# Loading a fused attention and gMLP kernel in smaller pieces: x tiles one by one, q weights in four blocks, k weights between two halves of x block 1

## The chip, the cores and the metric

The kernel runs on one core of a Trainium2 chip. The metric is the time of one execution on the device in microseconds (us). Five runs of the kernel before are at hand, and one execution recorded by the hardware profiler.

The engines are named as in the profile: PE is TensorE's matmul, PEld its weight load, DVE is VectorE, ACT is ScalarE, POOL is GpSimd, SP is SyncE (it only issues transfers here). A trailing q (SPq, ACTq) is an engine's instruction queue.

## What is computed

One input x (2048 tokens of 512 features, bf16) is normalised, and the sum of x, a local attention branch and a gated MLP branch is returned.

```python
xn = layernorm(x)                                   # over 512 features
# A: 32 heads of 16; each token attends to 8 tokens, 2 apart, itself and back
q, k, v = split(xn @ wqkv)                          # wqkv: 512 x 1536
attn = softmax(mask(q . k[pos - 2*w] * 16**-0.5), over w = 0..7)
A = (sum over w of attn * v[pos - 2*w]) @ wo
# B: gMLP with a token-mixing matrix
z = gelu(xn @ w_in)                                 # 512 x 1376, two halves of 688
z2 = layernorm(z[:, 688:])
B = (z[:, :688] * (w_sp @ z2 + b_sp)) @ w_out       # w_sp: 2048 x 2048
out = x + A + B
```

## The kernel before

The 2048 tokens stand as 16 tiles of 128 tokens. Tile i = 4*tb + j belongs to block j (0 to 3) and to row group tb (0 to 3), so a block is four tiles that are 512 tokens apart. `xall[:, j, tb]` holds tile (j, tb) of x, tokens on the partitions. A tile goes through these steps:

- `ln_stats` (L205, L206, DVE): mean and variance of each token.
- `ln_sqrt` (L209, ACT) and `ln_recip` (L212, DVE): 1/sqrt(var + eps).
- `ln_apply` (L216, DVE): the normalised tile, in place.
- transposed into `xnT` (features on the partitions): either `tr` (L223, four PE transposes into PSUM) and `tr_copy` (L227, ACT), or `tr_dma` (L231, a transposing transfer issued by SP). Block 0 and the first two tiles of block 1 go through PE, the other ten tiles by DMA.

`qk_part(pq, j, m, b0, b1)` (L308) then multiplies the transposed tiles b0 to b1 of block j with a quarter of the q or k weights: m = 0, 1 are the q weights `wqk[:, 0]`, m = 2, 3 the k weights `wqk[:, 1]`. `qk_copy` (L318, ACT) casts a finished product to SBUF, where DVE multiplies q with shifted k (L342). The products for z follow at L237.

The order of instructions on PE, DVE, ACT, SP and POOL is written out by hand (`manual_schedule`). In the opening part, the lines L557 to L641 give it; from there on the token list `ORDER` gives it, and the change touches nothing in that list. The framework adds the waits. It also gives the transfers eight completion semaphores in turn, in the program's order: the ninth transfer uses the first one again, and its issuing queue waits until the older transfer has landed.

What the opening does, in the program's order:

- Loads (L171 to L180). Tiles 0 and 1 of block 0 come as column halves of 64 KB, the left ones issued by SP, the right ones by ACT. ACT then issues tiles 2 and 3 of block 0 as one transfer of 256 KB. SP issues the q weights (512 KB), block 1 of x (512 KB), the k weights (512 KB), blocks 2 and 3 of x, and the z2 weights `w_z2` (688 KB).
- `warm_up` (L550): ten matmuls on zeros while the first data arrive, two more after the first transposes.
- Tiles 0 and 1 of block 0 are normalised and transposed, then tiles 2 and 3.
- PE multiplies q for tiles 0 and 1 (the products `pqs[0]`, `pqs[1]`), with the transposes of tiles 2 and 3 between; then q for tile 2 alone (`qk_part(..., 2, 3)`, L583 and L584), then k for tiles 0 and 1 (`pqs[2]`, L585: the first use of the k weights), then q for tile 3 alone (L595).
- ACT copies `pqs[0]` and `pqs[1]` out, and then takes the square root for tiles 2 and 3 of block 1 (L597), which go through `ln_apply` and `tr_dma`.

Of the kernel before, what the change touches and what calls it, by code (L numbers as in the profile page):

```python
# [15 lines left out]
P = 128  # L16
S = 2048
D = 512
NT = S // P
TB = 4  # L20
TBS = 512
C = D // P
# [48 lines left out]
def kernel(  # L71
# [14 lines left out]
    A = nc.scalar  # L86
    G = nc.gpsimd
    PE = nc.tensor
    SP = nc.sync
# [3 lines left out]
    xblk = x2.rearrange("(b j p) d -> j p b d", b=TB, j=4)  # L93
# [9 lines left out]
    xall = r_x[:, 0:4 * TB * D].rearrange("p (j b d) -> p j b d", j=4, b=TB)  # L103
    vp = r_x[:].rearrange("p (d t) -> p d t", d=DH)
    r_w = sb.tile([P, 8192], BF16, name="r_w")
    wqk = r_w[:, 0:4096].rearrange("p (s k f) -> p s k f", s=2, k=C)
# [57 lines left out]
    def load_x0(E, tb, h):  # L164
        E.dma_start(xall[:, 0, tb, 256 * h:256 * h + 256], x2[tb * TBS:tb * TBS + P, 256 * h:256 * h + 256])

    def load_wqk(E, s):
        E.dma_start(wqk[:, s],
                    A_wqkv[:, s * D:(s + 1) * D].rearrange("(k p) f -> p k f", p=P))

    for tb in range(2):  # L171
        load_x0(SP, tb, 0)
        load_x0(A, tb, 1)
    A.dma_start(xall[:, 0, 2:4, :], xblk[0][:, 2:4, :])
    load_wqk(SP, 0)
    SP.dma_start(xall[:, 1], xblk[1])
    load_wqk(SP, 1)
    for j in range(2, 4):
        SP.dma_start(xall[:, j], xblk[j])
    SP.dma_start(w_z2[:], B_w_in[:, FH:F].rearrange("(k p) f -> p k f", p=P))  # L180
# [121 lines left out]
    def qk_part(pq, j, m, b0, b1, ccs=(0, 1), p0=None, kcs=range(C)):  # L302
        sd, c0 = m // 2, 2 * (m % 2)
        p0 = b0 if p0 is None else p0
        xv = xnT[:].rearrange("p k (b j t) -> p k b j t", b=TB, j=4)
        for cc in ccs:
            for kc in kcs:
                PE.matmul(pq[:, cc, p0 * P:(p0 + b1 - b0) * P], wqk[:, sd, kc, c0 + cc:D:C],  # L308
                          xv[:, kc, b0:b1, j, :], start=(kc == 0), stop=(kc == C - 1))

    def qk_copy(pq, j, m, b0=0, b1=TB, p0=None):
        sd, c0 = m // 2, 2 * (m % 2)
        p0 = b0 if p0 is None else p0
        if sd == 0:
            dst = qs[:, j, c0:c0 + 2, b0 * P:b1 * P].rearrange("p c (b t) -> p c b t", b=b1 - b0)
        else:
            dst = ks[:, c0:c0 + 2, HALO:HALO + S].rearrange("p c (b j t) -> p c b j t", b=TB, j=4)[:, :, b0:b1, j, :]
        cast = A.copy(dst, pq[:, :, p0 * P:(p0 + b1 - b0) * P].rearrange("p c (b t) -> p c b t", b=b1 - b0))  # L318
        if sd == 1:
            for i in k_reads[j]:  # L320
                tc.declare_no_dep(cast.ins, i, reason="other token columns of the same rows")
            k_casts[j].append(cast.ins)

    def qk_tile():
        return ps_mm.tile([P, 2, TBS], F32, name="pq", tag="mm")
# [250 lines left out]
    pqs = [qk_tile() for _ in range(3)]  # L576
# [3 lines left out]
    qk_part(pqs[1], 0, 1, 0, 2, (0,))  # L580
    tr_copy(t0[3], tr(t0[3]))
    qk_part(pqs[1], 0, 1, 0, 2, (1,))
    qk_part(pqs[0], 0, 0, 2, 3)  # L583
    qk_part(pqs[1], 0, 1, 2, 3)  # L584
    qk_part(pqs[2], 0, 2, 0, 2)  # L585
    for n in range(2):
        ln_stats(i1[n])
# [4 lines left out]
    ln_apply(i1[1])  # L592
    ln_stats(i1[3])
    for n in range(2):
        qk_part(pqs[n], 0, n, 3, 4)  # L595
        qk_copy(pqs[n], 0, n)
    ln_sqrt(slice(9, 16, 4))  # L597
    ln_stats(i2[0])
# [22 lines left out]
    pqs = [qk_tile() for _ in range(3)]  # L621
# [79 lines left out]
```

## Time and profile before

| what | value |
|---|---|
| median of 5 runs | 203.96 us (203.88 to 204.41) |
| the profiled execution: time, span of the instructions in it | 204.89 us, 203.2 us |
| granted TensorE clock | 1.000 |
| PE, DVE, ACT busy, share of the span | 97%, 92%, 49% |
| bytes read from HBM, written to it | 10.13 MB, 2.10 MB |
| q weights: issue, packets from and to, landed | 1.73, 2.87 to 6.07, 6.99 us |
| x tiles 2 and 3 of block 0 | 1.74, 3.56 to 6.49, 7.11 us |
| x block 1 | 2.20, 6.07 to 7.52, 8.61 us |
| k weights | 2.75, 7.53 to 9.01, 10.11 us |
| x block 2 | 3.31, 9.02 to 10.51, 11.62 us |
| x block 3 | 4.48, 10.53 to 12.05, 13.07 us |
| w_z2 | 5.08, 12.05 to 14.31, 14.89 us |

The transfers' times are those of the profiled execution, in microseconds from the first instruction: the start of the issuing instruction, the starts of the first and the last data packet (packets put to transfers by their order in the queue), and the last of the sixteen marks with which a transfer reports its landing. A row of a timeline or of the groups gives line, engine, operation, the names written and read, the shape and a count; brackets at its end give the idle time ahead of it and what ended it. PE rows overlap, since a matmul's time includes its way through the array: the pace is read from start to start.

### The profile page before, as it was taken

What the parts mean: (1) busy time and instruction counts of PE and PEld (TensorE: products, weight loads), DVE (VectorE), ACT (ScalarE), POOL (GpSimd) and SP (SyncE); (2) the same over time, 40 slices, a digit from 0 to 9 for tenths busy, and PEclk for the clock granted to TensorE, in tenths of its full rate; (3) what the DMA queues carried; (4) which work ended last, traced back from release to release, by engine and by line L of the source; (5) the groups of instructions that cost most, each with busy time, mean ns of one, the idle gap of its engine ahead of it and who ended that gap; (6) DMA issues with size and microseconds to landing.
All of it is one profiled execution on the core that took longest, in us unless ns stands there. A gap on an engine that the chain in (4) does not pass through costs nothing.

```text
span 203.2 us, 4070 instructions
## 1 busy us (share of the span) xinstructions
PE 196.9 (97%) x1687; PEld 125.0 (62%) x1691; DVE 187.1 (92%) x267; ACT 100.1 (49%) x162; POOL 11.5 (6%) x14
## 2 busy tenths in 40 slices
PE   7799999999999999999999999999999999999993
PEld 2498866565566666666556666666546645664562
DVE  5689899999999999999989998999999999999804
ACT  3466999999969984651642309647100210031000
POOL 3000000593000000000000000000000000000000
PEclk9999999999999999999999999999999999999999
DMA  4982448100198000687398966989927810744264
GB/s 130 361 270 53 89 99 206 60 0 3 42 193 181 3 0 0 114 205 171 30 219 200 189 169 105 205 163 162 183 50 194 212 43 0 216 102 93 55 194 135
DMA packets 66290, 25.91 MB, mean 128 GB/s; under 512 B 56224, under 2 KB 66016, under 8 KB 66016
## 3 DMA queue, kind: packets, MB, share of 16 engines
q1 hardware_dynamic: 65568, 25.19, 55.0%
q10 hardware_dynamic: 704, 0.47, 0.7%
q8 instruction: 13, 0.21, 0.5%
q14 instruction: 5, 0.04, 0.1%
HBM read 10.13 MB, written 2.10 MB: 60 GB/s over the span
## 4 chain that ended last, share of the span: by engine, by line
PE 89%; DMA 4%; DVE 2%; SPq 2%; issue 1%; ACTq 0%; DVEq 0%
PE pg L451 37%; PE pz L237 18%; PE pq L308 13%; PE pv L412 7%; PE po L523 6%; PE po L499 5%; DMA r_x<-in_A_x_dram 3%; SPq L476 1%; PE pl L362 1%; DVE r_qk L513 1%; DMA out_dram<-r_qk 1%; PE po L508 1%; DVE stats L205 1%; PE pt L223 1%; PE pa L308 0%
## 5 line engine op out<-in xcount | busy, mean ns | idle before, releaser
L451 PE MATMUL pg<-z,r_qk 128*128 128x344 bf16 x448 | 67.3, 309 | 0.0
L451 PEld LDWEIGHTS <-r_qk 128*128 128x128 bf16 x448 | 43.7, 98 | 22.4 <-issue 0.8
L237 PE MATMUL pz<-w_z,xnT 128*128 128x344 bf16 x256 | 40.1, 309 | 0.0
L426 DVE TENSOR_TENSOR r_pr<-r_x,r_w 128x2048 bf16<-128x2048 bf16 x32 | 38.3, 1221 | 0.3
L430 DVE TENSOR_TENSOR r_pr<-r_pr 128x2048 bf16<-128x2048 bf16 x28 | 33.9, 1219 | 0.2
L457 ACT ACTIVATE gs<-pg,b_col 128x688 bf16<-128x688 f32 x16 | 13.3, 832 | 40.6 <-PE pg L451 25.1
L237 PEld LDWEIGHTS <-xnT 128*128 128x128 bf16 x256 | 24.9, 98 | 13.4 <-issue 0.8
L308 PE MATMUL pq<-xnT,r_w 128*128 128x256 bf16 (+2 forms) x192 | 28.8, 304 | 0.2 <-DMA r_w<-in_A_wqkv_dram 0.2
L342 DVE TENSOR_TENSOR r_pr<-r_qk 128x2048 bf16<-128x2048 bf16 x24 | 28.5, 1222 | 0.0
L308 PEld LDWEIGHTS <-r_w 128*128 128x128 bf16 x200 | 20.2, 114 | 7.4 <-DMA r_w<-in_A_wqkv_dram 0.7
L299 ACT ACTIVATE r_uz<-pz 128x688 bf16<-128x688 f32 x16 | 11.5, 742 | 22.5 <-PE pz L237 22.3
L318 ACT CAST r_qk<-pq 128x1024 bf16<-128x1024 f32 (+1 forms) x16 | 15.3, 990 | 2.4 <-PE pq L308 2.3
L523 PE MATMUL po<-r_w,r_uz 128*128 128x512 bf16 x66 | 14.9, 379 | 0.6 <-issue 0.6
L513 DVE TENSOR_TENSOR r_qk<-po,r_qk 128x512 bf16<-128x512 f32 x14 | 9.2, 687 | 6.2 <-PE po L523 6.0
L412 PE MATMUL pv<-xnT,r_w 128*32 128x512 bf16 x256 | 14.6, 380 | 0.0
L499 PE MATMUL po<-r_lg,r_pr 32*128 32x512 bf16 x224 | 14.5, 375 | 0.0
L523 PEld LDWEIGHTS <-r_uz 128*128 128x128 bf16 x85 | 8.0, 98 | 9.8 <-issue 1.5
L351 DVE TENSOR_TENSOR r_pr<-r_pr 128x4096 bf16<-128x4096 bf16 x6 | 13.7, 2290 | 0.0
L205 DVE BATCH_NORM_STATS2 stats<-r_x 128x6 f32<-128x512 bf16 (+1 forms) x18 | 10.8, 612 | 2.5 <-DMA r_x<-in_A_x_dram 2.5
L261 ACT ACTIVATE junk<-z 128x688 bf16<-128x688 bf16 x16 | 12.5, 778 | 0.2
L412 PEld LDWEIGHTS <-r_w 128*32 128x32 bf16 x256 | 9.4, 138 | 4.6 <-issue 0.3
L255 ACT ACTIVATE z<-pz 128x688 bf16<-128x688 f32 x16 | 11.8, 739 | 0.8 <-PE pz L237 0.8
(81 smaller groups left out, 176.4 us busy)
## 6 DMA issues: line engine op xcount, KB each, us to landing
r_lg<-in_A_wo_dram SPq DMA_DIRECT2D x8, 256.0 KB, 4.0
r_qk<-in_A_x_dram SPq DMA_DIRECT2D x16, 128.0 KB, 2.3
out_dram<-r_qk SPq DMA_DIRECT2D x15, 128.0 KB, 2.0
r_w<-in_A_wqkv_dram SPq DMA_DIRECT2D x3, 512.0 KB, 5.1
r_x<-in_A_x_dram SPq DMA_DIRECT2D x3, 512.0 KB, 6.4
w_z<-in_B_w_in_dram SPq DMA_DIRECT2D x2, 688.0 KB, 5.8
r_w<-in_B_w_out_dram SPq DMA_DIRECT2D x1, 640.0 KB, 6.3
r_x<-in_A_x_dram ACTq DMA_DIRECT2D x1, 256.0 KB, 5.4
```

The source lines that it names most:

```text
L237: PE.matmul(pz[:, hh, 0:FHALF], xnT[:, kc, i * P:(i + 1) * P], wz[:, kc, hh * FHALF:(hh + 1) * FHALF], start=(kc == 0), stop=(kc == C - 1))
L308: PE.matmul(pq[:, cc, p0 * P:(p0 + b1 - b0) * P], wqk[:, sd, kc, c0 + cc:D:C], xv[:, kc, b0:b1, j, :], start=(kc == 0), stop=(kc == C - 1))
L318: cast = A.copy(dst, pq[:, :, p0 * P:(p0 + b1 - b0) * P].rearrange("p c (b t) -> p c b t", b=b1 - b0))
L342: prod = V.tensor_tensor(pr[g % 3][:, c].rearrange("p w b t -> p b w t"), q3.unsqueeze(2).broadcast_to([P, TB, 4, P]), k4, ALU.mult)
L351: V.tensor_tensor(pr[g % 3][:, 0:2], pr[g % 3][:, 0:2], pr[g % 3][:, 2:4], ALU.add)
L412: PE.matmul(pv[32 * tb:32 * tb + 32, dd, :], wv[:, kc, 2 * d2 + dd, :], xnT[:, kc, tb * TBS:(tb + 1) * TBS], start=(kc == 0), stop=(kc == ...
L426: V.tensor_tensor(pw_t[n], vp[:, :, off:off + P], a_sb[:, slot_w(w), ts].unsqueeze(1).broadcast_to([P, DH, P]), ALU.mult)
L430: V.tensor_tensor(pw_t[n] if dst is None else dst, pw_t[n], pw_t[m], ALU.add)
L451: PE.matmul(pg[:, hh, 0:FHALF], wsp[n][:, k, :], z2[:, k, hh * FHALF:(hh + 1) * FHALF], start=(k == 0), stop=(k == NT - 1))
L457: A.activation(gs[:], tiles.pop(("g", n))[:, :, 0:FHALF], ACT.Identity, bias=b_col[:, i:i + 1])
L499: PE.matmul(pc, op[32 * tb:32 * tb + 32, d, o * P:(o + 1) * P], wo_r[32 * tb:32 * tb + 32, d, cs], start=(d == 8), stop=False, tile_positi ...
L523: PE.matmul(pc, uT[:, o % 2, m, tb * P:(tb + 1) * P], wout[:, m, cs], start=False, stop=(m == MCH - 3))
```

## The change

The two single transfers of 256 KB and 512 KB at the start become pieces, and x block 1 is cut around the k weights.

- x tiles 2 and 3 of block 0 come as two transfers of 128 KB, both issued by ACT.
- The q weights come as four transfers of 128 KB, one for each 128 rows of the matrix (`k`, the contraction blocks that a matmul of `qk_part` uses one at a time).
- Of x block 1, tiles 0 and 1 are loaded one by one ahead of the k weights, tiles 2 and 3 one by one behind them.
- On PE, the q products of tile 2 and of tile 3, two groups of 16 matmuls with 128 columns, become one group of 16 matmuls with 256 columns. It stands where that of tile 3 stood, behind the first use of the k weights.

Tiles 0 and 1 of block 0 are loaded as before. The other engines' instructions keep their order.

```diff
-    def load_wqk(E, s):
-        E.dma_start(wqk[:, s],
-                    A_wqkv[:, s * D:(s + 1) * D].rearrange("(k p) f -> p k f", p=P))
+    def load_wqk(E, s, k0=0, k1=C):
+        E.dma_start(wqk[:, s, k0:k1],
+                    A_wqkv[:, s * D:(s + 1) * D].rearrange("(k p) f -> p k f", p=P)[:, k0:k1])
 
     for tb in range(2):
         load_x0(SP, tb, 0)
         load_x0(A, tb, 1)
-    A.dma_start(xall[:, 0, 2:4, :], xblk[0][:, 2:4, :])
-    load_wqk(SP, 0)
-    SP.dma_start(xall[:, 1], xblk[1])
+    for tb in range(2, TB):
+        A.dma_start(xall[:, 0, tb], xblk[0][:, tb])
+    for k in range(C):
+        load_wqk(SP, 0, k, k + 1)
+    for tb in range(2):
+        SP.dma_start(xall[:, 1, tb], xblk[1][:, tb])
     load_wqk(SP, 1)
+    for tb in range(2, TB):
+        SP.dma_start(xall[:, 1, tb], xblk[1][:, tb])
     for j in range(2, 4):
         SP.dma_start(xall[:, j], xblk[j])
...
     qk_part(pqs[1], 0, 1, 0, 2, (1,))
-    qk_part(pqs[0], 0, 0, 2, 3)
-    qk_part(pqs[1], 0, 1, 2, 3)
     qk_part(pqs[2], 0, 2, 0, 2)
...
     for n in range(2):
-        qk_part(pqs[n], 0, n, 3, 4)
+        qk_part(pqs[n], 0, n, 2, 4)
         qk_copy(pqs[n], 0, n)
```

## The prediction

> **What bounds the kernel now.** I read the engine table first, then the chain of waits in order of time, then the rows of the first 16 us on each engine, then the DMA rates of the same stretch. The engine table names TensorE (PE), 97% of the span.
>
> ```profile
> PE 196.9 (97%) x1687; PEld 125.0 (62%) x1691; DVE 187.1 (92%) x267; ACT 100.1 (49%) x162; POOL 11.5 (6%) x14
> ```
>
> So an edit pays only where it moves PE's unbroken stream. The chain (start, length, what) shows where that stream begins:
>
> ```profile
> 1.74 5.37 DMA r_x<-in_A_x_dram
> 7.11 0.03 issue
> 7.13 0.70 DVE stats L205
> ...
> 9.39 0.40 PE pt L223 x4
> 9.79 0.44 PE pq L308 x4
> 10.22 0.22 PE pt L223 x4
> 10.45 3.53 PE pq L308 x48
> ```
>
> The 256 KB transfer of x tiles 2 and 3 comes first, then the statistics of tile 2 on VectorE (DVE), then its transpose on PE at 9.39. From there to 191.57 the chain is PE's, but for 0.5 us called issue. What happens before 9.39 therefore counts one for one, as long as nothing later becomes late. Three timelines show what stood idle:
>
> ```profile
> 5.33 0.41 DVE L216 TENSOR_SCALAR r_x<-r_x,mv,rstd 128x512 bf16<-128x512 bf16 x1
> 7.13 0.69 DVE L205 BATCH_NORM_STATS2 stats<-r_x 128x6 f32<-128x512 bf16 x1 [1.39 <-DMA r_x<-in_A_x_dram]
> ```
>
> ```profile
> 7.03 1.06 PE L308 MATMUL pq<-xnT,r_w 128*128 128x256 bf16 x8 [0.18 <-DMA r_w<-in_A_wqkv_dram]
> 9.39 0.40 PE L223 MATMUL pt<-ident,r_x 128*128 128x128 bf16 x4 [1.29 <-DVE r_x L216]
> ```
>
> ```profile
> 5.97 1.14 ACT L227 COPY xnT<-pt 128x512 bf16<-128x512 bf16 x3 [0.90 <-PE pt L223]
> 8.08 0.30 ACT L209 ACTIVATE rstd<-mv,eps_t 128x1 f32<-128x1 f32 x1 [0.97 <-DVE mv L206]
> ```
>
> DVE lost 1.39 us to the transfer, and PE lost 1.29 us to DVE. The rates (last column GB/s, one row per microsecond) say why the data came late:
>
> ```profile
> 3.00:4.00 1.00, 1.00 (x3) 0.29 (x2) 0.97 (x4) 0.59 (x2) 0.00 (x0) 1.00 0.46 62
> 4.00:5.00 1.00, 1.00 (x4) 0.29 (x2) 0.93 (x5) 0.43 (x2) 0.00 (x0) 1.00 0.92 300
> ...
> 7.00:8.00 1.00, 0.97 (x8) 0.80 (x8) 0.84 (x3) 0.11 (x1) 0.00 (x0) 1.00 1.09 354
> ```
>
> After a thin start the engines run full until 13 us, near 350 GB/s. In that stretch it is the order of the bytes that decides who waits.
>
> **Tiles 2 and 3 one by one.** ScalarE (ACT) issues two transfers of 128 KB where it issued one of 256 KB. One more issue costs about 0.45 us of its queue (the two half tiles took 0.90), so the table load moves from 2.22 to about 2.68 and ends at 3.96, not 3.50. The first square root ran at 3.92: it moves by some 0.05 us, and its reader, the reciprocal at 4.66, stands behind DVE's second statistics anyway. Price nothing; without that cover, 0.05.
>
> DVE can start tile 2's statistics at 5.66 (as at 9.44 and 9.77, the next row starts 0.33 after an apply starts), if tile 2 has landed. It wants tile 3 0.83 later, at 6.49. When do they land? By packet starts, the before kernel has moved 512 KB by 4.7 and 768 KB by 5.4. In the new order those are the halves plus tile 2 and q block 0, then tile 3 and q block 1. Landing marks came 0.6 to 0.9 after the last packet (tiles 2 and 3: 6.49, then 7.11; q weights: 6.07, then 6.99). That gives 5.3 to 5.6 and 6.0 to 6.3, both in time. Upper bound for each: 7.11, as before. I take in time, since every byte count is lower than before.
>
> The gain at DVE is then 7.13 - 5.66 = 1.47. One thing is next late: tile 2's square root on ACT stands behind the third copy (start 6.72, and the copy before it started 0.26 earlier). It runs from 7.00 to 7.30, so the reciprocal goes to 7.32 where 8.75 - 1.47 would be 7.28. The net gain is 1.43, and tile 2 is transposed at 7.96. PE is free by then: its eight q matmuls can start at about 6.87 after the second copy and take 8 x 0.109.
>
> **Q weights in four blocks.** The last byte of q was needed at 7.03 and landed at 6.99. In the new order 1,024 KB end with q block 3, and the before kernel passed that count at 6.1, so it lands at 6.7 to 7.0. It is wanted when the third copy is done, at 7.11: no loss. The queue pays: SyncE (SP) issues 128 KB in about 0.41 to 0.45 us, so x block 1 and the k weights are issued later. The program gives transfers eight completion semaphores in turn, and a reused one makes SP wait for the older transfer. Blocks 2 and 3 and the two x tiles wait for the four half tiles (landed 2.86 to 3.54): issued at about 3.1, 3.6, 4.05 and 4.5. The k weights wait for tile 2: issued at 4.95 if it has landed, against 2.75. Behind that wait on SP stand the rest of x and w_z2. SP delivers 128 KB per 0.45 us, 290 GB/s, a little under the 350, with ACT's 256 KB beside it; I put starvation at 0 to 0.3 us.
>
> The Trainium skill speaks against such pieces: "DMA: Bandwidth & Descriptors" (Anatomy of one DMA, and Rules for kernel authors) gives about 2.0 us fixed plus bytes/436 GB/s per transfer, and advises to coalesce many small ones. As an estimate from that page, four blocks one after another would take 4 x 2.3 = 9.2 us and end near 10.9, nearly 4 us late. The trace differs where it can: SP's two half tiles were issued 0.45 us apart and landed 0.50 apart (2.86, 3.36), each 2.05 to 2.10 after its issue. The fixed part overlaps, so I go by that row.
>
> **The k weights and PE's order.** The diff takes the 32 matmuls of 128 columns that did tiles 2 and 3 singly and makes 16 of 256. Row by row 32 x 0.056 = 1.79 becomes 16 x 0.109 = 1.74: 0.05 saved. More important, 16 of them (10.72 to 11.62) stood ahead of the first use of the k weights and now stand behind it. PE reached them at 10.72; 1.43 earlier is 9.29, and that is when it now wants k. Before, k landed at 10.11, with 1.5 us to spare. Now 256 KB less go ahead of it (half of x block 1): 0.262 MB / 350 GB/s = 0.75, so 9.36. If the thin stretch from 3 to 4 us fills up by half, it is 8.9. Both ends: 8.9 gives no wait, 10.11 a wait of 0.82. I take 9.3, no wait.
>
> **What follows.** The next PE landmark is the 512-column group at 14.70: 14.70 - 1.43 - 0.05 = 13.22. The first q copy on ACT moves from 13.13 to about 11.2, because both halves of tile group 0 finish sooner. With it go the square root at 14.95, DVE's 0.60 us wait behind it and SP's transposes of tiles 2 and 3 of block 1 from 15.94, all by about 1.9. PE wanted those at 19.92 and had them at 19.77; that margin grows. x block 1's last tiles, now behind k, land at 9.4 to 10.2 and are wanted at 9.95 and 11.57; x block 2 has the same bytes ahead as before (11.62, wanted at 12.39). DVE meets PE's copies again at its 0.73 us wait at 24.07, so both streams enter the steady part 1.48 earlier, and all later work there is released by one or the other.
>
> The sum: -1.43 -0.05 = -1.48. The profiled execution took 204.89 (span 203.20 and 1.69 around it), so 203.41 for it. The median of the runs is 203.96, 0.93 below the profiled one: 202.48, say 202.5. Anything over 0.2%, 0.41 us, can be told from no change here.
>
> **Rivals.**
> 1. Data only partly earlier: tile 3 or k land where they did. Tile 3 at 7.11 costs 0.62; k at 10.11 costs 0.82. One of them gives 203.1 to 203.3. For: the margins are 0.1 to 0.3 us. Against: fewer bytes go ahead of each.
> 2. No change: tile 2 also lands at 7.11, because ACT's queue got going late before (its first packet came at 3.56, for an issue at 1.74). Then DVE starts where it did, k has time, and only 0.05 is left: 203.9.
> 3. Slower, by the k weights alone: SP holds them for tile 2. If that lands at 7.11, k is issued at 7.15; with the 5.3 us that the q weights took from issue to landing it lands at 12.45. PE would want it at 9.29 to 10.72 and stand: a loss of 1.7 net, 205.6. The point of decision is a landing at 10.77 (9.29 + 1.48); beyond 11.18 the loss can be measured. For: two queued waits and later issues. Against: the engines are full, so a transfer's landing is set by the bytes ahead, not its issue.
>
> **The numbers.** Forecast 0.62 (202.3 to 202.8), rival 1 0.20, rival 2 0.07, rival 3 0.11. The range 202.2 to 203.5 takes in the forecast, rival 1 and a little scatter of the runs (203.88 to 204.41 before). Faster 0.82, same 0.07, slower 0.11.
>
> **What would show it.** Right: DVE's 1.39 us idle row ahead of tile 2 gone or under 0.1; PE's transposes of tile 2 near 7.96; no PE wait for r_w near 9.3; the 512-column group near 13.2; the sequence from 25 us on like before, 1.48 earlier; span 201.7. Wrong: an idle row on PE released by r_w at the first k matmuls, a DVE wait for x before tile 3 or tiles 2 and 3 of block 1, or a new wait after 25 us that gives the gain back.

## The result and the profile after

The changed kernel is slower, not faster. Its median is 204.92 us over 44 runs (203.92 to 206.66), against 204.21 us for the kernel before on the same chips. The ratio is 1.0038, with a 95% interval of 1.0027 to 1.0049. The forecast was 202.5. The profiled execution took 205.57 us with a span of 203.9, where the prediction's sum for it was 203.41 and 201.7.

The share of PE in the engine table has not moved, so the place to look is again the chain of waits (start, length, what):

```profile
4.67 5.71 DMA r_w<-in_A_wqkv_dram
10.38 0.04 issue
10.42 3.25 PE pq L313 x28
```

Where x tiles 2 and 3 stood before, the k weights stand now. The timeline of DVE shows that the first step of the prediction came true: the idle row ahead of tile 2 is gone.

```profile
5.83 0.69 DVE L210 BATCH_NORM_STATS2 stats<-r_x 128x6 f32<-128x512 bf16 x1
...
10.70 0.69 DVE L210 BATCH_NORM_STATS2 stats<-r_x 128x6 f32<-128x512 bf16 x1 [0.47 <-DMA r_x<-in_A_x_dram]
```

The timeline of PE shows what took its place. The brackets give the idle time ahead of a row and what ended it.

```profile
8.15 0.40 PE L228 MATMUL pt<-ident,r_x 128*128 128x128 bf16 x4
...
9.05 0.60 PE L313 MATMUL pq<-xnT,r_w 128*128 128x256 bf16 x4
10.42 3.25 PE L313 MATMUL pq<-xnT,r_w 128*128 128x256 bf16 x28 [0.77 <-DMA r_w<-in_A_wqkv_dram]
...
14.39 0.81 PE L313 MATMUL pq<-xnT,r_w 128*128 128x512 bf16 x3
```

Tile 2 is transposed 1.24 us earlier than before (9.39 to 8.15). PE then reaches the k weights at 9.65 and stands until 10.42. The 512-column group starts at 14.39: 0.31 earlier than before, where 1.48 was forecast. Its row in the profile before:

```profile
14.70 4.51 PE L308 MATMUL pq<-xnT,r_w 128*128 128x512 bf16 x32
```

The DMA rates fell in just the stretch in which the pieces move (one row per microsecond, last column GB/s):

```profile
5.00:6.00 1.00, 1.00 (x7) 0.38 (x6) 0.96 (x4) 0.24 (x1) 0.00 (x0) 1.00 0.91 221
6.00:7.00 1.00, 1.00 (x7) 0.63 (x7) 0.97 (x3) 0.91 (x3) 0.00 (x0) 1.00 0.87 255
7.00:8.00 1.00, 1.00 (x9) 0.77 (x7) 0.93 (x4) 0.75 (x3) 0.00 (x0) 1.00 0.88 239
```

The first two of these rows in the profile before:

```profile
5.00:6.00 1.00, 1.00 (x9) 0.60 (x8) 0.70 (x3) 0.10 (x2) 0.00 (x0) 1.00 1.07 370
6.00:7.00 1.00, 0.85 (x6) 0.35 (x4) 0.00 (x0) 1.00 (x3) 0.00 (x0) 1.00 1.08 377
```

So the new loads get ahead and then fall behind: up to 4.0 they had moved 0.52 MB, where it was 0.34, and up to 8.0 1.52 MB, where it was 1.74.

The 0.31 us kept in the opening stayed to PE's end (199.72, where it was 200.03), and then more was given back behind it. In the last output group, DVE's second add waits for an output store, so that its buffer comes free. The row of after, and then that of before:

```profile
199.40 0.69 DVE L518 TENSOR_TENSOR r_qk<-po,r_qk 128x512 bf16<-128x512 f32 x1 [1.13 <-DMA out_dram<-r_qk]
```

```profile
198.77 0.69 DVE L513 TENSOR_TENSOR r_qk<-po,r_qk 128x512 bf16<-128x512 f32 x1 [0.18 <-DMA out_dram<-r_qk]
```

So every execution can be read as a sum of four parts. The first is the opening, up to the first 512-column group. The second is PE's stream from there to its last matmul. The tail runs from there to DVE's last add, and the rest to the last instruction. The stream took 185.32 to 185.34 us in 17 of the 20 profiles of this study, whatever the kernel; it was longer in e4 (185.47), h3 (185.59) and h2 (186.85). In the other 17 only the opening and the end differ. The two kernels' profiles divide like this:

| | opening | PE's stream | tail | rest | span |
|---|---|---|---|---|---|
| before | 14.70 | 185.33 | 0.69 | 2.45 | 203.2 |
| after | 14.39 | 185.33 | 1.64 | 2.50 | 203.9 |

### The profile page after: what moved, and what is told of

Same layout as the page of the kernel before. It is cut to its first block, busy times and chain, and to the rows that moved or that the text cites. A ratio compares the mean times of both kernels' runs of the same rounds, so it can differ in the third digit from the quotient of the medians.

```text
span 203.9 us, 4043 instructions
## 1 busy us (share of the span) xinstructions
PE 197.2 (97%) x1671; PEld 125.0 (61%) x1675; DVE 187.2 (92%) x267; ACT 100.0 (49%) x162; POOL 11.3 (6%) x14
## 4 chain that ended last, share of the span: by engine, by line
PE 91%; DMA 5%; SPq 1%; DVE 1%; issue 1%; DVEq 0%
PE pg L456 37%; PE pz L242 18%; PE pq L313 12%; PE po L528 7%; PE pv L417 7%; PE po L504 6%; DMA r_w<-in_A_wqkv_dram 3%; PE pl L367 1%; DMA r_x<-in_A_x_dram 1%; DMA out_dram<-r_qk 1%; PE po L513 1%; PE pb L504 1%; DVE r_qk L518 1%; PE pa L313 0%; SPq L179 0%
## 5 line engine op out<-in xcount | busy, mean ns | idle before, releaser
L313 PE MATMUL pq<-xnT,r_w 128*128 128x256 bf16 (+1 forms) x176 | 28.9, 316 | 0.8 <-DMA r_w<-in_A_wqkv_dram 0.8
```

## The experiments

The theories have letters in the expectations. For the opening: **K**: PE's wait for the k weights is the loss; the new loads bring k late and the new PE order wants it early. **O**: the PE order alone is the loss. **P**: the 128 KB pieces starve the transfer engines. P was first written down ahead of g1 and f2, K and O under these letters ahead of h1 to h4. For the end, a transfer issue on SP was seen to be held up by a refill of PE's instructions. Three theories, written down ahead of the first runs (e1 to e4), say why it hit the changed kernel: **A**, its 16 fewer PE instructions move the refill there; **B**, its other number of transfers does; **C**, it scatters from execution to execution.

This table gives all kernels with a profile each, and the texts below refer to it. Loads: "old" as before, "new" as in the change. Order: PE's order, old or new. Stores: two output stores of the last groups on SP's queue (as in both kernels) or on ACT's. "k marks" are the first and the last of the sixteen marks with which the k weights report their landing; "wait" is PE's idle time ended by them. The ratio is to the kernel before on the same chip in the same series of runs, with its 95% interval.

| kernel | loads | order | stores | ratio | opening | k marks | wait | tail |
|---|---|---|---|---|---|---|---|---|
| before | old | old | SP | 1 | 14.70 | 9.03 to 10.11 | 0 | 0.69 |
| before_a | old | old | SP | one run | 13.90 | 9.00 to 9.45 | 0 | 0.78 |
| t1_two_stores_act | old | old | ACT | 0.9987 (0.9971 to 1.0003) | 13.38 | 9.11 to 9.55 | 0 | 0.43 |
| e2_pe_order_only | old | new | SP | 1.0016 (0.9996 to 1.0035) | 13.76 | 9.05 to 9.75 | 0.19 | 1.37 |
| h1_pe_order_act | old | new | ACT | 1.0001 (0.9989 to 1.0013) | 14.07 | 9.04 to 9.63 | 0 | 0.43 |
| e1_loads_only | new | old | SP | 1.0023 (1.0000 to 1.0047) | 13.29 | 8.21 to 10.07 | 0 | 0.87 |
| h2_loads_act | new | old | ACT | 1.0003 (0.9981 to 1.0026) | 13.72 | 8.66 to 10.56 | 0.25 | 0.43 |
| after | new | new | SP | 1.0038 (1.0027 to 1.0049) | 14.39 | 8.68 to 10.38 | 0.77 | 1.64 |
| e3_two_groups_late | new | new, tiles singly | SP | 1.0041 (1.0019 to 1.0063) | 13.98 | 8.62 to 9.92 | 0.20 | 1.43 |
| a1_after_stores_act | new | new | ACT | 1.0025 (1.0010 to 1.0040) | 14.74 | 8.47 to 10.72 | 1.14 | 0.43 |
| e4_k_ahead | new, k ahead of x block 1 | new | SP | 1.0019 (1.0004 to 1.0035) | 13.52 | 7.39 to 9.11 | 0 | 0.81 |
| h3_k_ahead_act | the same | new | ACT | 1.0007 (0.9995 to 1.0020) | 14.20 | 7.76 to 9.87 | 0 | 0.43 |
| h4_k_behind_act | new, k behind x block 1 | new | ACT | 1.0114 (1.0080 to 1.0148) | 17.17 | 9.72 to 11.49 | 2.11 | 0.43 |
| f1_tiles_only | old, tiles 2, 3 one by one | old | SP | 0.9992 (0.9980 to 1.0003) | 14.54 | 9.07 to 9.76 | 0 | 0.56 |
| c2_tiles_act | the same | old | ACT | 1.0024 (1.0010 to 1.0037) | 14.43 | 9.32 to 9.72 | 0 | 0.43 |
| f2_q_blocks_only | old, q in four | old | SP | 1.0045 (1.0026 to 1.0063) | 13.59 | 9.01 to 10.35 | 0 | 0.92 |
| f2 again | the same | old | SP | 1.0032 (1.0011 to 1.0052) | 14.53 | 8.95 to 11.37 | 0.93 | 0.98 |
| g1_q_in_one | new, q in one | new | SP | 1.0083 (1.0062 to 1.0105) | 13.77 | 8.22 to 9.75 | 0.10 | 1.23 |
| g1 again | the same | new | SP | 1.0052 (1.0033 to 1.0072) | 14.12 | 8.36 to 9.42 | 0 | 1.27 |
| c1_loads_q_one_act | new, q in one | old | ACT | 1.0007 (0.9997 to 1.0018) | 14.13 | 8.11 to 9.33 | 0 | 0.43 |

The repeats of f2 and g1 differ from their first runs by 0.0013 and 0.0031, and f1 and c2, which differ in their stores alone, by 0.0032. A difference of some 0.003 between kernels of two series therefore proves little. The firm comparisons are those within one series.

### One half of the change at a time

The loads without the new PE order:

```diff
+    qk_part(pqs[0], 0, 0, 2, 3)
+    qk_part(pqs[1], 0, 1, 2, 3)
     qk_part(pqs[2], 0, 2, 0, 2)
...
-        qk_part(pqs[n], 0, n, 2, 4)
+        qk_part(pqs[n], 0, n, 3, 4)
```

> The new loads with the order of before on PE (q for tile 2, 16 matmuls of 128 columns, again ahead of the first use of the k weights). All theories: tile 2 is transposed near 8.15 us as in the changed kernel; PE reaches the k weights about 0.9 us later than there (near 10.5 instead of 9.65), so that a landing near 10.4 costs nothing and PE's steady stream runs about 1.05 us ahead of before. Theory A (what is lost at the end hangs on the number of PE instructions, which moves PE's 16 KB instruction refills against SP's transfer issues): PE has the old number again, the end is that of before, 203.15 us, 1.05 faster. Theory B (it hangs on the seven more transfers, which shift SP's instructions, semaphores and rings): the end is late as in the changed kernel, 204.1 to 204.2, no change. Theory C (the refill's length is chance, and the two profiled executions differ by that alone): near 203.2.

The PE order without the loads, put into the kernel before:

```diff
-    qk_part(pqs[0], 0, 0, 2, 3)
-    qk_part(pqs[1], 0, 1, 2, 3)
...
-        qk_part(pqs[n], 0, n, 3, 4)
+        qk_part(pqs[n], 0, n, 2, 4)
```

> The loads of before with PE's new order (one group of 16 matmuls with 256 columns behind the first k products). All theories: PE wants the k weights at 10.72, they land at 10.1 as before, so no wait; the stream runs 0.05 us ahead. Theory A: 32 PE instructions fewer put the refills where the changed kernel has them, and the end is late by 0.7 to 1.0: 204.9 to 205.2. Theory B: the transfers are those of before: 204.15. Theory C: 204.15.

The changed kernel with tiles 2 and 3 in two single groups, still in the late place:

```diff
-        qk_part(pqs[n], 0, n, 2, 4)
+        qk_part(pqs[n], 0, n, 2, 3)
+        qk_part(pqs[n], 0, n, 3, 4)
```

> The changed kernel, with the merged group as two groups of 128 columns again, in its late place. It has the old number of PE instructions from there on, and every load of the changed kernel. All theories: PE waits for the k weights for about 0.77 us as in the changed kernel, and the stream is 0.27 ahead of before (0.32 less 0.05). Theory A: the end is that of before: 203.95. Theory B: the end stays late: 204.95, as the changed kernel. Theory C: 203.95 to 204.3.

The changed kernel with the k weights ahead of the two tiles of x block 1:

```diff
+    load_wqk(SP, 1)
     for tb in range(2):
         SP.dma_start(xall[:, 1, tb], xblk[1][:, tb])
-    load_wqk(SP, 1)
```

> The changed kernel with the k weights ahead of the two tiles of x block 1 again. All theories: 256 KB less ahead of k, so it lands 0.7 to 1.0 us earlier, near 9.5, and PE's 0.77 us wait is gone or under 0.2; the two x tiles land later, 9 to 10 instead of 8.85 at the latest, and DVE, which wants the first at 8.53, waits 0.5 to 1.3 us for them without PE waiting. PE's stream 0.9 to 1.1 ahead of before. Theory A and theory B: late end as in the changed kernel, 204.1 to 204.3. Theory C: 203.2 to 203.4.

All four ratios lie between 1.0016 and 1.0041 and their intervals overlap; none shows the forecast gain. e1 has the best opening of any kernel with pieces (13.29, close to the 13.22 that the prediction gave to the whole change). Its PE has 16 matmuls of 128 columns to do while k is on its way, as before, and does not stand. In e3, with PE's instructions as many as before, k is waited for again:

```profile
9.97 1.23 PE L313 MATMUL pq<-xnT,r_w 128*128 128x256 bf16 x11 [0.20 <-DMA r_w<-in_A_wqkv_dram]
```

The tails speak against A and B. e2 has the new number of PE instructions and the old number of transfers, e3 the old number of instructions and the new number of transfers, and both have the long tail (1.37 and 1.43); e4, with both numbers of the changed kernel, has 0.81. C is left, with one profile of each kernel; it is not shown. Its times were missed too: it put e1 near 203.2, e3 at 203.95 to 204.3 and e4 at 203.2 to 203.4, and the medians are 204.32, 205.08 and 204.53. B's times came within 0.25 us of all four medians, though the tails are not where B has them.

### The end taken out

SP issues the four reloads of x for the last output group ahead of the store that DVE's add waits for. The issue timelines of before and of after, four transfers of 128 KB in one row:

```profile
193.77 2.81 SPq L476 DMA_DIRECT2D r_qk<-in_A_x_dram  x4
```

```profile
193.45 3.54 SPq L481 DMA_DIRECT2D r_qk<-in_A_x_dram  x4
```

Three of the four take 0.43 each. The second takes 1.38 (before) and 2.10 us (after). At its start one of PE's 16 KB instruction transfers begins, which the trace lists as a queue of its own. Before, that transfer lasts to 195.27 and the issue to 195.63; after, to 195.67 and to 196.04. To take this out, two output stores go to ACT's queue, so that they no longer stand behind the reloads:

```diff
-             ... "s": out_store, "end": last_adds,
+             "s": lambda o, tb: out_store(o, tb, 0, A if o == 2 and tb in (1, 2) else SP), "end": last_adds,
```

In the kernel before:

> The kernel before; two of the third group's output stores (row groups 1 and 2) are issued by ACT instead of SP, where they stand behind four reloads of x, one of which is held by PE's last instruction refill. Theory C (the end's length hangs on how long that refill takes, 1.0 to 1.7 us in the profiles so far): the store lands by 194, DVE's add of row group 1 in the last group no longer waits for it, the last add ends 0.4 to 0.5 us after PE's last matmul (0.69 in the profile of before, 0.8 to 1.6 in the others): 203.6 to 203.8, 0.4 to 0.6 faster, and less scatter. Rival (the end is bound by PE or by the reloads themselves): 204.2, no change. For the opening: its loads are those of before, so by the theory that the recorded execution of before was an unlucky one, x tiles 2 and 3 land near 5.8 and not at 7.1.

In the changed kernel:

> The changed kernel with the same two stores on ACT. Theory C: the end's 0.95 us is gone, 204.9 goes to 204.0 to 204.2, about the time of before; what is left against the former run is the wait for the k weights (0.4 to 0.8 us on PE's row). Rival (the end is not what makes the changed kernel slower): 204.7 to 204.9.

The wait is gone in both; t1's timeline of DVE shows the two adds in one row:

```profile
196.57 1.29 DVE L513 TENSOR_TENSOR r_qk<-po,r_qk 128x512 bf16<-128x512 f32 x2 [5.02 <-PE po L523]
```

The tail is 0.43 in all eight kernels with these stores. It is worth about the same on both sides: the kernel before goes from 1 to 0.9987, the changed one from 1.0038 to 1.0025; neither step is clear of its intervals. t1 and a1 ran in one series. They stand at 203.89 and 204.77, 0.88 us apart with equal tails (and equal streams, 185.33 and 185.32). a1's expectation by C, 204.0 to 204.2, failed, and the rival's 204.7 to 204.9 was met. So the changed kernel's loss is not the end. By the two profiles it lies in the opening (13.38 and 14.74). a1's timeline of PE shows the wait for k:

```profile
10.77 3.25 PE L313 MATMUL pq<-xnT,r_w 128*128 128x256 bf16 x28 [1.14 <-DMA r_w<-in_A_wqkv_dram]
```

### How much there was to gain

The kernel before, with tiles 2 and 3 one by one and nothing else:

```diff
-    A.dma_start(xall[:, 0, 2:4, :], xblk[0][:, 2:4, :])
+    for tb in range(2, TB):
+        A.dma_start(xall[:, 0, tb], xblk[0][:, tb])
```

> The kernel before with x tiles 2 and 3 of block 0 one by one (the first part of the change alone). By the prediction's step: tile 2 is there at 5.66, 1.4 us faster, 202.8. By the theory of the unlucky execution: before had no such wait in most executions, so 204.0 to 204.3, no change; k lands as before, near 10.

It makes no difference that can be told: 0.9992. Tile 2 is now in time, and tile 3 is not, for which DVE waits 1.05 us (and PE then 1.43 for tile 2's transposes):

```profile
7.76 0.69 DVE L206 BATCH_NORM_STATS2 stats<-r_x 128x6 f32<-128x512 bf16 x1 [1.05 <-DMA r_x<-in_A_x_dram]
```

A second execution of the kernel before, and t1, whose loads are the same, answer a question that one profile could not.

> The kernel before, unchanged, for a second profile. Theory of the unlucky execution: x tiles 2 and 3 land near 5.8 and DVE's statistics of tile 2 start by 5.9 with no idle time ahead of them; the 512-column group starts at 13.3 to 13.6 instead of 14.70, and the span is 201.8 to 202.6. Rival (the first profile is typical): landing at 7.1, idle 1.39, span 203.2.

Their rows for tile 2 on DVE, before_a and then t1:

```profile
6.33 0.69 DVE L205 BATCH_NORM_STATS2 stats<-r_x 128x6 f32<-128x512 bf16 x1 [0.58 <-DMA r_x<-in_A_x_dram]
```

```profile
5.74 0.68 DVE L205 BATCH_NORM_STATS2 stats<-r_x 128x6 f32<-128x512 bf16 x1
```

With the same loads, tiles 2 and 3 landed at 7.11, 6.30, 5.38, 5.83 (e2) and 6.52 (h1), and DVE's wait was 1.39, 0.58, 0, 0 and 0.77: 0.55 in the mean. The execution that the prediction was read from was the worst of the five.

### The same with a clean end, and the dose

The next four kernels ran in one series and have the two stores on ACT. h1 is e2, h2 is e1 and h3 is e4 with them.

> The loads of before, PE's new order, and the two output stores on ACT, so that the end is clean (last add 0.43 after PE). Theory K (what makes the changed kernel slower is PE's wait for the k weights, which come later through the pieces and are wanted earlier through PE's order): k lands at 9.5 to 10.1 with the old loads, PE wants it at 9.3 to 10, waits 0 to 0.3; time about that of the same kernel with the old order (0.9987 of before), 203.7 to 204.1. Rival O (PE's new order is the loss by itself): 204.5 or more.

> The changed loads, PE's old order (16 matmuls ahead of the first use of k again), the two stores on ACT. Theory K: k as late as in the changed kernel, 9.9 to 10.7, but wanted near 10.5, wait 0 to 0.2; 203.7 to 204.1, that is 0.9990 to 1.0005 of before. Rival L (the pieces cost time elsewhere too, by DVE's wait for x block 1): 204.4 to 204.8, as the changed kernel with the two stores on ACT (1.0025).

> The changed kernel with the k weights ahead of x block 1 and the two stores on ACT. Theory K: k by 9.1 to 9.6, no PE wait; DVE waits 0.5 to 1 us for x block 1 off PE's path; 203.8 to 204.2. Rival L: 204.4 to 204.8.

h4 moves the k weights the other way, behind all of x block 1:

```diff
-    load_wqk(SP, 1)
     for tb in range(2, TB):
         SP.dma_start(xall[:, 1, tb], xblk[1][:, tb])
+    load_wqk(SP, 1)
```

> The changed kernel with the k weights behind all four tiles of x block 1 (256 KB more ahead of them) and the two stores on ACT. Theory K: k lands 0.7 to 1.0 us later still, at 10.8 to 11.6, PE waits 1.2 to 2.0 us, and the time rises by as much as k does, to 205.3 to 205.8 (1.005 to 1.008 of before). Rival L: as the changed kernel with the stores on ACT, 204.5 to 204.9.

h1, h2 and h3 are level with the kernel before (1.0001, 1.0003, 1.0007), h4 is 1.14% slower. h4's timeline of PE, and then its table by microsecond, in which the third number from the end is the granted PE clock:

```profile
11.54 4.92 PE L313 MATMUL pq<-xnT,r_w 128*128 128x256 bf16 x28 [2.11 <-DMA r_w<-in_A_wqkv_dram]
```

```profile
11.00:12.00 1.00, 0.46 (x4) 0.43 (x5) 1.00 (x3) 0.00 (x0) 0.00 (x0) 0.92 1.09 369
12.00:13.00 1.00, 1.00 (x6) 0.69 (x5) 0.41 (x2) 0.00 (x0) 0.00 (x0) 0.50 1.07 367
13.00:14.00 1.00, 1.00 (x6) 0.75 (x5) 0.88 (x2) 0.00 (x0) 0.00 (x0) 0.50 1.06 371
14.00:15.00 1.00, 1.00 (x7) 0.69 (x6) 0.00 (x0) 0.05 (x1) 0.00 (x0) 0.50 0.43 151
15.00:16.00 1.00, 1.00 (x10) 0.92 (x9) 0.00 (x0) 0.96 (x1) 0.00 (x0) 0.87 0.07 26
```

In these two executions PE's wait for k sets the time: k 0.77 later than in a1 (11.49 against 10.72) makes the opening 2.43 longer. Of that, 0.77 is the wait itself, and 1.66 is new: after 2.11 us without work PE's clock fell to half for some 3.4 us (0.16, 3 whole ones and 0.26 by the column), and the same matmuls from the first k product to the 512-column group took 5.63 us and not 3.97. The expectation, 205.3 to 205.8, was passed by far (the median is 207.01). The halved clock is not all of it: two other executions of h4, of 206.56 and 206.86 us, show a mean granted clock of 1.000, where the profiled one shows 0.992. That each half of the change alone costs little, and both together 0.25%, fits K and speaks against O. It is not shown beyond doubt: a1's interval overlaps those of h1 and h2, and they are from two series. In h3, which loads k ahead, PE did not wait for k, but DVE did for x block 1 (and PE 0.56 us for the last block of q, landed at 8.17), so the wait was moved and not removed:

```profile
10.25 0.69 DVE L210 BATCH_NORM_STATS2 stats<-r_x 128x6 f32<-128x512 bf16 x1 [1.72 <-DMA r_x<-in_A_x_dram]
```

h2's profiled execution was one of its long ones (205.22 us, median 203.97): PE stood there for the transposed tiles of x block 1. Its x tiles had landed at 10.90 and 11.25, and ACT's square root for them, at 13.97, followed ACT's copies without a gap. The issue of the first transposing transfer took 2.00 us on SP (1.30 before), beside a 16 KB instruction transfer from 15.44 to 16.54, and the last mark of the second came 1.03 us behind its first (0.15 before).

```profile
20.44 3.69 PE L313 MATMUL pq<-xnT,r_w 128*128 128x256 bf16 x32 [1.34 <-DMA xnT<-r_x]
```

### Which pieces do it

f2 is the kernel before with the q weights in four blocks:

```diff
-    load_wqk(SP, 0)
+    for k in range(C):
+        load_wqk(SP, 0, k, k + 1)
```

> The kernel before with the q weights as four transfers, nothing else (the second part of the change alone). Theory P: the rate from 4 to 7 us falls under 320 GB/s and k, with the same bytes ahead as before, lands 0.3 to 0.8 us later than before's 9.45 to 10.11, at 10.0 to 10.6; PE wants it near 10.3 to 10.7 in this order, so a wait of 0 to 0.3; time 204.2 to 204.6, same or slightly slower. Rival: k near 9.7, time 204.1.

g1 is the changed kernel with the same lines the other way:

> The changed kernel with the q weights as one transfer of 512 KB again (x tiles, x block 1 cut around k, and PE's order stay). Theory P (128 KB pieces, issued 0.47 us apart by SP, keep the transfer engines short of work: 220 to 300 GB/s from 5 to 8 us where the kernel before had 354 to 377): the rate from 5 to 8 us goes back to about 340 or more, k lands at 9.0 to 9.5 and not at 9.9 to 10.7, PE's wait for it falls from 0.2 to 1.1 us to under 0.2, and the time is 204.2 to 204.5. Rival (k is late because of the slowest engine's lag, whatever the pieces): k near 10.2, time 204.8.

c1 is e1 with q in one transfer and the two stores on ACT, c2 is f1 with the two stores on ACT:

> A candidate: the changed loads but q in one transfer, PE's order of before (q for tile 2 ahead of k), and the two output stores on ACT. Theory P and theory C together: tile 2's statistics at 5.7 to 5.9 without a wait, no PE wait for k, the 512-column group at 13.3 to 13.5, the last add 0.43 after PE's end: 203.3 to 203.7, 0.4 to 0.9 faster than before. Rival: the scatter of the landings eats it, 203.9 to 204.2.

> A second candidate: the loads and order of before but x tiles 2 and 3 one by one, and the two output stores on ACT. Tile 2 at 5.8, tile 3 by 6.5 to 7.7 (it was 7.74 in the one profile of the split alone, with a wait): 203.5 to 203.8.

c1 and c2 were tried as versions that might beat both kernels. Neither does.

The blocks of q alone, with all else as before, lose 0.45%. The one profile of f2 didn't show why, and g1 was slower than any theory had it, so both were taken up again:

> The kernel before with the q weights as four row blocks (everything else as before) and the two output stores on ScalarE. With the stores left on SP the blocks alone gave 1.0045, although the one profile showed an opening (512-column group at 13.59) as early as that of others. Theory E (the end made that loss, by an instruction refill that holds SP): with the stores moved it goes, ratio 0.9987 to 1.000, last add 0.43 us behind PE's end. Theory P (the pieces starve the transfer engines and the k weights come late in some executions, which one profile need not show): it stays above 1.0025.

> The changed kernel with the q weights in one transfer again, and the two output stores on ScalarE. With the stores left on SP it gave 1.0083, with k at 9.75 and a wait of 0.10 us on PE, but with an output store that landed 0.9 us late at the very end. Theory K (PE's wait for the k weights is the loss, and the four q pieces are what delays k): k lands at 9.4 to 9.8, PE waits 0 to 0.2 us, ratio 0.9985 to 1.001, clearly below the 1.0025 of the changed kernel with the same stores. Rival (the q pieces do no harm; PE's order with any late k does): 1.0025 as with the pieces. Rival E2 (the loss of g1 lies in the stream, not in its end): 1.006 to 1.008 again.

The two kernels that ran under these labels left the stores on SP. They are second runs of f2 and g1, so the part of the expectations that rests on the stores was not tried. What they do show is another execution of each. f2's is the clearest sight of the cost of the pieces: with PE's old order, and its 16 filler matmuls, PE still stood for k.

```profile
11.41 2.40 PE L309 MATMUL pq<-xnT,r_w 128*128 128x256 bf16 x28 [0.93 <-DMA r_w<-in_A_wqkv_dram]
```

The landing marks say how. Five executions with the old loads and five with the new ones (after, e3, a1, e1, h2) have their first mark of k at 9.00 to 9.11 and at 8.21 to 8.68: the new order does bring the first of them earlier (in after by 0.35, where the forecast moved k by 0.75). The last mark comes 0.44 to 1.08 later with the old loads, and 1.30 to 2.25 later with the new ones. The lag builds up over the pieces, and stays (first and last mark):

| transfer | before_a | after |
|---|---|---|
| q weights | 6.02 to 6.49 | blocks: 4.18 to 4.69, 4.98 to 5.88, 5.31 to 6.66, 5.66 to 6.98 |
| x block 1 | 7.51 to 7.95 | tile 0: 6.00 to 7.31, tile 1: 6.64 to 8.85 |
| k weights | 9.00 to 9.45 | 8.68 to 10.38 |
| x block 2 | 10.51 to 10.96 | 10.83 to 12.59 |

Some of the sixteen DMA engines run up to 2.4 us behind the others (the second f2), and a transfer has landed when the last of them has. The Trainium skill states that rule in "DMA: Bandwidth & Descriptors" (Why a DMA increments its semaphore by 16 and not by 1): the engines finish independently and only the full count of 16 means that all has landed. The marks of this case agree. From 4 to 8 us the rate was 350 to 365 GB/s in the five executions with the old loads, and 250 to 312 in the five with the new ones. In the second f2 it stood at 267, 255 and 247 in the three microseconds from 5 on; h1, with the old loads, had 374, 363 and 346.

With q in one transfer (g1 and c1), k's last mark is at 9.75, 9.42 and 9.33, in time or nearly so. What P says of the blocks of q holds for the opening, then: with them the rate falls and k is late. That too little had been issued is not shown: in after, 1.31 MB ahead of the k weights had been issued by 4.62, and 1.03 MB had been moved by 6.0. Why the engines slow down and drift apart is open; the trace at hand doesn't name the engine of a packet.

g1 doesn't fit K: k in time, and yet the slowest after h4. Its two profiles have openings of 13.77 and 14.12 and so no reason there, but long ends: tail and rest together are 4.58 and 3.94 us, against 3.14 before. In the first, the last output store has its first mark at 201.71 and its last at 202.61, beside an instruction transfer of 8 KB; in the second, the add of the last group waits for its store again. That the instruction transfers make all of its loss is not shown: no run took them away.

## Why the prediction was wrong

**The gain at DVE (-1.43).** The mechanism is right: tile 2's statistics follow their apply without a gap (5.83, forecast 5.66; the first half tiles had landed 0.17 later). The tiles landed earlier than forecast (4.50 and 5.71, forecast 5.3 to 5.6 and 6.0 to 6.3). The size was wrong for the comparison that counts. 1.39 us of idle time was read from one execution and taken from the median of all, though the mean over five executions with these loads is 0.55. The text itself noted that the profiled execution lay 0.93 above the median, and subtracted the two as if they were independent.

**The k weights (9.3, no wait).** This is the step that failed and turned the sign: k landed at 10.38, not at 9.36, and PE stood 0.77 us for it. The 9.36 was k's old landing, 10.11, less 0.75 for the 256 KB that no longer go ahead of it. That took the old pace of the engines and the old lag for granted, and the "starvation" of 0 to 0.3 was left out of it. The last packet would have gone out at 8.26 (9.01 less 0.75); it went out at 9.05, since the engines moved 250 GB/s from 4 to 8 us, not 350. That is 0.79 of the miss of 1.02. The landing then came 1.33 us behind that packet, not 1.10 as before: 0.23 more. The sentence that landing marks come 0.6 to 0.9 after the last packet was itself short, since for k and for x blocks 1 and 2 the table before has 1.09 to 1.11. The upper bound of 10.11, with its wait of 0.82, was too low by 0.27 for after and 0.61 for a1.

**The q blocks (starvation 0 to 0.3).** They landed where forecast (6.98, in 6.7 to 7.0), and did PE no harm; the harm fell on the transfers behind them (f2 has the blocks alone, and k at 10.35 and 11.37). The Trainium skill's advice in "DMA: Bandwidth & Descriptors" (Rules for kernel authors), to coalesce many small transfers, was set aside since the fixed part of a transfer overlaps. It does overlap: the last block landed nearly 4 us ahead of the estimate by that page, whose 2.0 us and 436 GB/s are given for transfers that GpSimd issues, while SP and ACT issue these. The advice was right all the same, by way of the lower rate and the lag.

**PE's order (-0.05, and k wanted 1.43 earlier).** PE wanted k at 9.48 by the prediction's own steps (8.15 plus 1.33), not 9.29, and got it at 10.42. The 16 matmuls moved behind were what had covered k's landing, 0.9 us of cover sold for 0.05.

**All later work 1.48 earlier.** PE's stream did follow its start, to a hundredth. The end was left out of the sum, as if it were rigid: the profiled executions differ there by 0.95 in the tail, which scatters (0.56 to 1.64 with the stores on SP).

For the profiled execution the miss is 205.57 - 203.41 = 2.16. Its parts: 0.19 for tile 2's later start, 0.94 for k, 0.95 for the tail, and 0.08 left.

**The rivals.** Rival 1's half on k is what happened (0.82 foreseen, 0.77 and 1.14 measured), but it was priced against a gain that the typical execution didn't have. Rival 3 had the right object, k late for PE. Its mechanism didn't act: SP issued k at 4.67, not at 7.15, and a later issue is not what made k late (e3 issued it at 5.21 and had it at 9.92). Its point of decision, a landing at 10.77, was nearly met by after and a1 (10.38, 10.72).

## What to carry to other kernels

A wait that one profiled execution shows is a gain only as far as other executions of the same kernel show it too; where the profiled run is slower than the median, look first whether the idle row to be removed is the reason. Cutting a transfer brings its first part earlier and the last mark of everything behind it later, so price the transfer behind the pieces at the lower pace and by its slowest engine, not by its bytes at the old pace. Work that stands ahead of a late operand is cover; don't move it away in the change that puts the operand under pressure.

## What the runs showed of the hardware

- In one execution a wait of 2.11 us was followed by half of PE's clock (h4: 0.50 from 12 to 15 us), while 1.14 (a1) and 1.34 (h2) left it at 1.00. The Trainium skill, in "TensorE: Matmul & The Clock Gate" (HAM oscillation — how this bites in real kernels), warns of gaps over some 3.4 us; here a shorter one did it, and the measurement decides.
- An issue of 128 KB on SP, 0.43 us as a rule, took 1.38 and 2.10 us where it met a 16 KB instruction transfer, and ended 0.36 to 0.37 us behind it.
- The same loads, byte for byte, landed tiles 2 and 3 anywhere from 5.38 to 7.11 us.
- The lowest ratio has the kernel before with two output stores on ACT's queue: 0.9987, with an interval from 0.9971 to 1.0003 that just takes in no change.
